# Attention with relative bias, then a snake MLP: the MLP lags one batch from the second batch on, and batch 1's attention output is transposed by DMA

## The chip, the cores and the metric

The kernel runs on one core of a Trainium2 chip. The metric is the device time of one execution in microseconds (us). The engines are TensorE (PE in the profile; PEld is its weight load), VectorE (DVE), ScalarE (ACT), GpSimd (POOL) and SyncE (SP), which here only issues DMAs. "Span" is the time from the first to the last instruction of the profiled execution.

## The reference

There are 8 batches of 8 heads, 576 positions and head size 64. All inputs are float32.

```python
scores = scale * np.matmul(q, k.transpose(0, 1, 3, 2))      # scale = 1/8
bias = bias_table[bucket]            # bucket depends on |i - j| alone, the last one from about 128 on
scores = scores + bias.transpose(2, 0, 1)[None, :, :, :]
scores = scores - np.max(scores, axis=-1, keepdims=True)
attn = np.exp(scores)
attn = attn / (np.sum(attn, axis=-1, keepdims=True) + 1e-09)
attn_out = np.matmul(attn, v)
...
x = np.ascontiguousarray(attn_out.transpose(0, 2, 1, 3)).reshape(B * S, H * D)   # 4608 x 512
h = x @ w_in                         # 512 -> 2048
s = np.sin(alpha * h)
g = h + s * s / (alpha + 1e-09)
return (g @ w_out).astype(np.float32)
```

## The kernel before

All matrix operands are float16. The attention works on one batch at a time and, within it, on four pairs of heads. The MLP works on nine blocks of 512 rows of x, which do not coincide with the 576 rows of a batch.

**Loads.** k and q of a batch from 2 on are first cast and rearranged from input to DRAM by GpSimd (`stage_kq`, two DMAs), and then loaded transposed into `kTs[t % 2]` and `qTs[t % 2]` by two DMA transposes on SyncE's queue, with two small copies of the last 64 keys into `kts` (`load_kqT`). v is loaded with a cast by six GpSimd DMAs (`load_v16`). For batch 2 the staging is issued in `first` of batch 0, and the loads in `first` of batch 1, which is executed where batch 1's first scores are emitted; there the staging of batch 3 follows on GpSimd's queue. For batches from 3 on, the function `ahead` (line 955) issues the loads, and the staging of the batch after, once the attention before last is finished. Batches 0 and 1 are loaded untransposed and transposed on TensorE (`plan_tr`).

**Attention.** `plan_qk` computes transposed scores: for a head pair p and a block i of 128 keys, two matmuls of 64 rows write one two-bank tile of PSUM; "t" is the last block of 64 keys of both heads together, and i = 4 the last 64 queries of four blocks. ScalarE takes the exponential into `u` (line 705), and VectorE multiplies it by the exponential of the bias near the diagonal (lines 713 and 730). `plan_av` multiplies `u` by v, to which a column of ones is attached, so that the sum of each row comes out too (24 exponentials, 36 product groups a batch). `norm` (lines 776 to 788) divides. The result must be transposed into `xT`, a ring of 1536 rows: for a batch that is not "far", TensorE transposes it (5 transposes for each head pair, line 822) and VectorE or ScalarE copies it (`put`, line 828); for a "far" batch `flip` (line 809) issues DMA transposes from `xp` on SyncE's queue. "Far" is `t >= LAG - 1`.

**PSUM.** Of eight banks, two are `am0` and `am1`, two each belong to regions R0 and R1 and two to region 2. Before batch LAG - 1 region 2 is two single banks, `ca` and `cb`, used by products, transposes and block 0's second matmul (tags "avE" and "moE"); scores then have two regions and are emitted tile by tile. From batch LAG - 1 on, region 2 is a third two-bank score tile (`c_mode` 2), and scores are emitted in the groups of lines 631 to 636, mostly two tiles at a time. The tile framework adds the waits where a region changes its form.

**MLP.** `plan_moe_in` computes h for a block in 16 tiles of four matmuls, in R0 and R1 with one bank each; ScalarE takes the sine, ScalarE or VectorE squares it, and VectorE makes g (line 879). `plan_mo` multiplies g by `w_out`: 4 x 16 matmuls for a block, called fills. Exponential and sine need different tables of ScalarE, so a switch costs an ACT_TABLE_LOAD, and the sines of a block wait for all exponentials ahead of them.

**Order.** `Plan.run` is a list scheduler that runs when the program is built. It takes the task that can start first by its own estimates of times; among those within 0.02 us it takes the one with the lowest priority number. The order in which it emits is the order of each engine's and each queue's program. Fills have the lowest urgency and fill gaps of TensorE; while scores of a batch are being emitted, `QUOTA` limits how many may go in: (a, b) allows a plus b times the share of the batch's score groups already emitted. Outside the scores they are not limited. The loop at line 945 plans, for each batch t, the attention, and then the MLP block `bs` of line 998; for t = LAG - 1 it plans no block, so that two attentions stand back to back. In the kernel before that is t = 2: the order is attention 0, block 0, attention 1, block 1, attentions 2 and 3, block 2, attention 4, block 3, and so on, and at the end blocks 6, 7 and 8. At t = LAG - 1 the tasks in `early` must also be done ahead of the first scores.

Of the kernel before, what the change touches and what calls it, by code (L numbers as in the profile page):

```python
# [20 lines left out]
def t_pe(n):  # L21
    return n / 2400.0 + 0.0025


def t_act(n):
    return n / 1200.0 + 0.052


def t_dve(n):
    return n / 960.0 + 0.07  # L30
# [141 lines left out]
WINDOW = 700  # L172
WARM_END = 30.0
FILL_GAP = 0.0
QUOTA = {2: (4, 26)}
QUOTA_ELSE = (8, 48)
LAG = 3
D_FLIP = 3.0
T_MODE = 0.11
T_START = 7.0  # L180
# [30 lines left out]
def kernel(  # L211
# [12 lines left out]
    T, H, S, D = q.shape  # L224
# [106 lines left out]
    def new_outs():  # L331
        return tp.tile([128, DM], F32, name="outs", tag="outs", bufs=NBUF["outs"])
# [29 lines left out]
    def bank(tag):  # L362
        if tag[:2] == "am":
            return new_ps(tag)
        n = its[tag]
        its[tag] += 1
        if tag == "avE":
            return new_c("ca") if n % 2 else new_ps("am0")
        if tag == "moE":
            return new_c("cb") if n % 2 else new_ps("am1")  # L370
        return new_c("ca" if n % 3 == 1 else "cb") if n % 3 else new_ps("am1")
# [3 lines left out]
    def stage_kq(t):  # L375
        for dst, src in ((staged_k, k), (staged_q, q)):
            nc.gpsimd.dma_start(  # L377
                out=dst.ap()[t].rearrange("s (h d) -> s h d", h=H),
                in_=src[t].rearrange("h s d -> s h d"),
            )  # L380
# [6 lines left out]
    def load_kqT(t):  # L387
        kT = kTs[t % 2]
        nc.sync.dma_start_transpose(out=kT[:, :, :], in_=staged_k.ap()[t])
        nc.sync.dma_start_transpose(out=qTs[t % 2][:, :, :], in_=staged_q.ap()[t])  # L390
        load_kt(t, 0, NP)

    def load_v16(t):
        vp = v[t].rearrange("h s d -> s h d")
        for c in range(4):
            nc.gpsimd.dma_start(  # L396
                out=vs[t % 2][:, c, :, 0:D], in_=vp[128 * c : 128 * c + 128],
            )
        vq = v[t].rearrange("(hp two) s d -> two s hp d", two=2)
        for z in range(2):  # L400
            nc.gpsimd.dma_start(
                out=vhs[t % 2][64 * z : 64 * z + 64, :, VC * z : VC * z + D], in_=vq[z, 512:S]
            )
# [45 lines left out]
    def full(out, lhsT, rhs, start, stop):  # L449
        nc.tensor.matmul(out=out, lhsT=lhsT, rhs=rhs, start=start, stop=stop)  # L450
# [83 lines left out]
    def copy_on(e, o, i):  # L534
        if e == "ACT":
            nc.scalar.activation(out=o, in_=i, func=AF.Copy)
        else:
            k_of(e).tensor_copy(out=o, in_=i)  # L538
# [84 lines left out]
    def plan_qk(t, deps, tails, first, gate, early):  # L623

        us, ubs = [Cell() for _ in range(NP)], [Buf("u") for _ in range(NP)]
        dones = [{} for _ in range(NP)]
        if t < LAG - 1:
            groups = [[(p, i)] for p in range(NP) for i in (0, 1, 2, 3, "t", 4)]
# [11 lines left out]
        for gi, g in enumerate(groups):  # L640
# [5 lines left out]
            def qk(e, gi=gi, g=g, scs=scs):  # L646
                if gi == 0:
                    first()
                    plan.in_qk, plan.used = True, 0
                    plan.quota = QUOTA.get(t, QUOTA_ELSE)  # L650
                plan.share = (gi + 1) / len(groups)
# [88 lines left out]
    avs, xps, xpn = {}, {}, {}  # L740

    def plan_av(t, p, w, u, ub, done):

        q0, n = WIN[w]
        nq = len(QC[w])
        at = "avE" if t < LAG - 1 else "am"
        ab, xb, tb = Buf(at), Buf("xn"), Buf(at)
        av, xn, tr = Cell(), Cell(), Cell()
        far = t >= LAG - 1
        if far:  # L750
# [86 lines left out]
    xdone = {}  # L837
# [65 lines left out]
    mo_last, cps = [], {}  # L903

    def plan_mo(b, a):

        mt = "moE" if b == 0 else "am" if b < T - 2 else "moL"
        mb, ob, m = Buf(mt), Buf("outs"), Cell()
        for f in range(NF):

            def mm(e, f=f):
                if f == 0:
                    m.v = bank(mb.tag)
                full(
                    m.v, gcell[b].v[:, f, 128 * a : 128 * a + 128], w_out16[:, f, :],
                    f == 0, f == NF - 1,
                )

            mo_last[:] = [plan.add({"PE": t_pe(512)}, mm, mo_last[:] + [gdone[(b, f)]],
                                   500000000 + 4 * b + a, nb=T_WO[f // 4] if b == 0 else 0.0,  # L920
                                   new=[mb] if f == 0 else [],
                                   use=[gbuf[b]] if f == 0 else [gbuf[b], mb])]
            mo_last[0].fill = True

        def cp(e):
            o = new_outs()
            copy_on(e, o, m.v)
            r0 = 512 * b + 128 * a
            nc.sync.dma_start(out=out[r0 : r0 + 128, :], in_=o)

        y = plan.add({"DVE": t_dve(512), "ACT": t_act(512)}, cp, mo_last[:], CP_PRI,
                     new=[ob], use=[mb])
        y.s_only = True
        cps.setdefault(b, []).append(y)

    def set_table(name):
        nc.scalar.preload_act_table_set(name)  # L937
        plan.sin = name == SIN_SET
# [6 lines left out]
    for t in range(T):  # L945
        PB = 1000000 * t

        def first(t=t):
            if t == 1:
                load_v16(t + 1)  # L950
                load_kqT(t + 1)
            if t < 2:
                stage_kq(t + 2)

        def ahead(e, t=t):
            load_kqT(t + 1)
            load_v16(t + 1)
            if t + 2 < T:
                stage_kq(t + 2)

        if 2 <= t < T - 1:
            aheads[t + 1] = plan.add({"SP": 0.1}, ahead, [], PB - 1000000,
                                     after=avs[t - 1] + xdone[(t - 1, 1)])
        if sins:
            gate = [plan.add({"ACT": D_TBL}, lambda e: set_table(EXP_SET), sins, PB)]
        sins = []
        deps, tails = [], []
        for p in range(NP):
            if t == 0 and p + 1 < NP:
                for kq in range(2):  # L970
                    tr[(0, p + 1, kq)] = plan_tr(0, p + 1, kq, 100 * (16 * p + 8), T_PAIR[p][kq])
            deps.append(pe_gate + (tr[(t, p, 0)][0] + tr[(t, p, 1)][0] if t < 2 else []))
            tails.append(tr[(t, p, 0)][1] if t < 2 else [])
            if (t, p) in split_of:
                tails[-1] = [split_of[(t, p)]]
        early = list(split_of.values()) if t == 1 else []
        if t in aheads:
            early = early + [aheads[t]]
        if t == LAG - 1:
            early = early + cps[0] + avs[1] + xdone[(1, 0)] + xdone[(1, 1)]  # L980

            def first(old=first):
                old()
                c_mode[0] = 2

        us, ubl, dones, exs = plan_qk(t, deps, tails, first, gate, early)
        exps = exps + exs
        for p in range(NP):
            for w in range(2):
                xdone.setdefault((t, w), []).extend(plan_av(t, p, w, us[p], ubl[p], dones[p]))  # L990
        if t == 0:
            for p in range(NP):
                for kq in range(2):
                    tr[(1, p, kq)] = plan_tr(1, p, kq, 20000 + 100 * kq + 10 * p, T_TR1[kq])
        if t == LAG - 1:
            continue
        tbl = [plan.add({"ACT": D_TBL}, lambda e: set_table(SIN_SET), exps, PB)]
        bs = [t] if t < LAG else [t - 1] if t < T - 1 else [t - 1, t, t + 1]
        for b in bs:
            m, s_ = plan_moe_in(b, tbl)  # L1000
            sins += s_
        exps = []
        pe_gate = [m]
        for b in bs:
            for a in range(4):
                plan_mo(b, a)
# [33 lines left out]
```

The softmax here doesn't subtract the row's maximum and nothing guards it: scores larger than these inputs give would overflow.

## Time and profile before

| what | us |
|---|---|
| median of 5 runs (range) | 392.82 (391.98 to 394.09) |
| the profiled execution, its own time | 392.62 |
| its span | 390.7 |
| PE busy | 377.3 (97%) |
| ACT busy | 323.6 (83%) |
| DVE busy | 262.2 (67%) |
| POOL busy | 81.8 (21%) |
| exponentials, line 705, 192 instructions | 157.4 |
| matmuls for h, 576 | 132.4 |
| products g, line 879, 144 instructions | 103.3 |
| sines, line 865, 144 instructions | 92.7 |
| transposes of x on TensorE, line 822, 40 | 5.0 |
| DMA transposes into xT, 64 | 2.9 each from issue to landing (median) |

A row of the page such as `PE 5989...` divides the span into 40 equal slices of 9.8 us; a digit is the busy share of a slice in tenths, 9 meaning 90% or more. In a timeline a row has start, duration, engine, line, operation, output<-input, shapes and a count; square brackets give the idle time before it and what ended it. Busy times of TensorE overlap at their ends, since a matmul of 512 columns starts every 0.216 us and is recorded with 0.38. Most matmuls carry line 450, that of a helper, so they are told apart by their tiles: `sc<-qT,kT` are scores, `am<-v,u` products with v, `sc<-xT,w_in` the h of the MLP, and `am<-w_out,g` (or `ca`, `cb`) fills.

### The profile page before, as it was taken

How to read it: one execution, taken by the hardware profiler on the slowest of the kernel's cores; microseconds unless marked ns; L12 is line 12 of the kernel's file. 1: busy time of each engine (PE TensorE's matmuls, PEld its weight loads, DVE VectorE, ACT ScalarE, POOL GpSimd, SP SyncE). 2: the span in 40 equal slices, each digit the busy share in tenths (PEclk: the TensorE clock that was granted, in tenths of full speed). 3: DMA queues.
4: the chain of work that ended last, by engine and by line, in shares of the span. 5: the costliest groups of instructions: out<-in, count | busy, mean ns of one | idle time of the engine just before them, and what ended most of it. 6: DMA issues, size and time to landing. Idle time of an engine off the chain costs nothing.

```text
span 390.7 us, 8566 instructions
## 1 busy us (share of the span) xinstructions
PE 377.3 (97%) x3401; PEld 189.4 (48%) x3401; DVE 262.2 (67%) x587; ACT 323.6 (83%) x458; POOL 81.8 (21%) x96
## 2 busy tenths in 40 slices
PE   5989999999999999999999999999999999999995
PEld 2466435644455554455445544564445444444442
DVE  3696977777676689667956895768676869429100
ACT  2886999988999999999989999999999969539211
POOL 5672863080005454002600400000000000000000
PEclk9999999999999999999999999999999999999999
DMA  9999999999928999992997498211014000020112
GB/s 169 210 208 219 207 172 144 167 152 132 147 67 90 155 153 161 158 155 54 141 167 107 60 67 187 59 21 42 29 42 60 17 28 29 27 81 2 61 73 81
DMA packets 148647, 41.99 MB, mean 107 GB/s; under 512 B 137784, under 2 KB 142992, under 8 KB 148608
## 3 DMA queue, kind: packets, MB, share of 16 engines
q0 software_dynamic: 89872, 19.04, 58.8%
q1 hardware_dynamic: 58512, 22.36, 31.4%
q8 instruction: 26, 0.43, 0.5%
q14 instruction: 13, 0.11, 0.1%
q10 hardware_dynamic: 224, 0.05, 0.1%
HBM read 37.76 MB, written 16.52 MB: 139 GB/s over the span
## 4 chain that ended last, share of the span: by engine, by line
PE 91%; ACT 4%; DVE 2%; DMA 1%; issue 1%; ACTq 0%; DVEq 0%
PE sc L450 44%; PE am L450 35%; PE cb L450 6%; PE ca L450 5%; ACT u L705 3%; DMA phi_sb<-phi_const 1%; PE cb L558 1%; DVE g L879 1%; PE am L558 1%; ACT s L865 1%; DVE kT L538 0%; DVE outs L538 0%; DVE xp L785 0%; PE ca L822 0%; ACT sq L872 0%
## 5 line engine op out<-in xcount | busy, mean ns | idle before, releaser
L705 ACT ACTIVATE u<-sc 128x1024 f16<-128x1024 f32 (+1 forms) x192 | 157.4, 898 | 12.8 <-PE sc L450 11.4
L450 PE MATMUL sc<-xT,w_in 128*128 128x512 f16 x576 | 132.4, 379 | 0.5 <-DVE g L879 0.5
L879 DVE SCALAR_TENSOR_TENSOR g<-sq,inv_a,sc 128x512 f16<-128x512 f16 x144 | 103.3, 746 | 22.0 <-PE am L450 14.7
L450 PE MATMUL am<-w_out,g 128*128 128x512 f16 x416 | 108.6, 380 | 0.3 <-DVE outs L538 0.2
L865 ACT ACTIVATE s<-sc,alphaT 128x512 f16<-128x512 f32 x144 | 92.7, 679 | 6.3 <-PE sc L450 4.8
L730 DVE TENSOR_TENSOR u<-u,m2r 128x512 f16<-128x512 f16 (+2 forms) x160 | 67.7, 438 | 30.9 <-ACT u L705 27.9
L450 PEld LDWEIGHTS <-w_in 128*128 128x128 f16 x576 | 55.2, 98 | 65.0 <-issue 1.6
L450 PEld LDWEIGHTS <-g 128*128 128x128 f16 x576 | 53.3, 98 | 64.1 <-issue 11.6
L450 PEld LDWEIGHTS <-u 128*128 128x128 f16 x1440 | 55.1, 97 | 18.7 <-issue 10.2
L450 PE MATMUL sc<-qT,kT 64*128 64x64 f16 (+1 forms) x512 | 50.3, 294 | 1.9 <-ACT u L705 0.9
L872 ACT ACTIVATE sq<-s 128x512 f16<-128x512 f16 x79 | 49.2, 628 | 2.3 <-DVE g L879 0.5
L450 PE MATMUL am<-v,u 128*128 128x65 f16 x1152 | 50.7, 193 | 0.0
L396 POOL DMA_DIRECT2D v<-in_v_dram x24 | 22.2, 1062 | 118.0 <-PE am L450 104.2
L874 DVE TENSOR_TENSOR sq<-s 128x512 f16<-128x512 f16 x65 | 27.4, 423 | 9.2 <-ACT s L865 8.8
L450 PE MATMUL am<-vh,u 128*128 128x130 f16 x144 | 32.1, 223 | 0.8 <-DVE xp L785 0.8
L450 PEld LDWEIGHTS <-kT 64*128 64x128 f16 x512 | 14.9, 95 | 28.6 <-issue 24.2
L785 DVE TENSOR_TENSOR xp<-am,rd 128x384 f16<-128x384 f32 (+1 forms) x48 | 23.6, 491 | 1.8
L784 DVE RECIPROCAL rd<-am 128x6 f32<-128x6 f32 (+1 forms) x56 | 10.5, 188 | 19.8 <-PE am L450 19.3
L450 PE MATMUL cb<-w_out,g 128*128 128x512 f16 x96 | 23.0, 379 | 0.0
L937 ACT ACT_TABLE_LOAD x13 | 16.7, 1283 | 0.2
L538 DVE COPY outs<-am 128x512 f32<-128x512 f32 x19 | 13.1, 688 | 4.3 <-PE am L450 4.1
L377 POOL DMA_DIRECT2D staged_q<-in_q_dram x6 | 15.1, 2515 | 3.7 <-DMA staged_q<-in_q_dram 3.7
(88 smaller groups left out, 175.2 us busy)
## 6 DMA issues: line engine op xcount, KB each, us to landing
out_dram<-outs SPq DMA_DIRECT2D x36, 256.0 KB, 2.2
staged_k<-in_k_dram POOLq DMA_DIRECT2D x6, 576.0 KB, 17.0
staged_q<-in_q_dram POOLq DMA_DIRECT2D x6, 576.0 KB, 21.8
v<-in_v_dram POOLq DMA_DIRECT2D x24, 128.0 KB, 8.3
w_in<-in_moe_w_in_dram POOLq DMA_DIRECT2D x4, 512.0 KB, 7.1
w_out<-in_moe_w_out_dram POOLq DMA_DIRECT2D x4, 512.0 KB, 10.9
w_out<-in_v_dram SPq DMA_DIRECT2D x4, 256.0 KB, 7.7
v1st<-in_v_dram POOLq DMA_DIRECT2D x4, 256.0 KB, 16.6
```

The costliest lines, as they stand in the source:

```text
L377: nc.gpsimd.dma_start(out=dst.ap()[t].rearrange("s (h d) -> s h d", h=H), in_=src[t].rearrange("h s d -> s h d"),)
L396: nc.gpsimd.dma_start(out=vs[t % 2][:, c, :, 0:D], in_=vp[128 * c : 128 * c + 128],)
L450: nc.tensor.matmul(out=out, lhsT=lhsT, rhs=rhs, start=start, stop=stop)
L538: k_of(e).tensor_copy(out=o, in_=i)
L705: nc.scalar.activation(out=o, in_=x, func=AF.Exp, scale=0.125)
L730: nc.vector.tensor_tensor(out=io, in0=io, in1=m2[:, 2 * p : 2 * p + 2, x0 : x0 + hi - lo], op=ALU.mult,)
L785: nc.vector.tensor_tensor(out=y.rearrange("p c (z d) -> p c z d", z=2), in0=a[:, :, :, 0:D], in1=r.unsqueeze(3).to_broadcast([128, nq, 2, ...
L865: nc.scalar.activation(out=s16.v, in_=h.v, func=AF.Sin, scale=alphaT[:, f : f + 1])
L872: nc.scalar.activation(out=sq.v, in_=s16.v, func=AF.Square)
L874: k_of(e).tensor_tensor(out=sq.v, in0=s16.v, in1=s16.v, op=ALU.mult)
L879: nc.vector.scalar_tensor_tensor(out=gcell[b].v[:, f, :], in0=sq.v, scalar=inv_a[:, f : f + 1], in1=h.v, op0=ALU.mult, op1=ALU.add,)
L937: nc.scalar.preload_act_table_set(name)
```

## The change

`LAG` becomes 2, and with it:

- The batch for which no block is planned is now t = 1. The order is attention 0, block 0, attentions 1 and 2, block 1, attention 3, block 2, and so on. From block 2 on it is that of before.
- Batch 1 becomes "far": its output is normalised into `xp` and transposed by DMA on SyncE's queue. Its scores are emitted in groups with three regions, and region 2 changes its form ahead of attention 1.
- The second matmul of block 0 uses `am0` and `am1` in place of `cb` and `am1`, since region 2 now belongs to scores.
- The first scores of batch 1, in place of those of batch 2, wait in the plan for the products and the transposed output of the batch ahead of them. They no longer wait for the output copies of block 0.
- The smaller quota (4, 26) for fills now holds for batch 1, and batch 2 has (8, 48).

```diff
@@ -172,9 +172,9 @@
-QUOTA = {2: (4, 26)}
+QUOTA = {1: (4, 26)}
 QUOTA_ELSE = (8, 48)
-LAG = 3
+LAG = 2
@@ -904,7 +904,7 @@
     def plan_mo(b, a):
 
-        mt = "moE" if b == 0 else "am" if b < T - 2 else "moL"
+        mt = "am" if b < T - 2 else "moL"
@@ -977,7 +977,7 @@
         if t == LAG - 1:
-            early = early + cps[0] + avs[1] + xdone[(1, 0)] + xdone[(1, 1)]
+            early = early + avs[t - 1] + xdone[(t - 1, 0)] + xdone[(t - 1, 1)]
```

## The prediction

> **What bounds the kernel now.** I read four views in this order: the page, the busy time of each engine by stage, the timelines of TensorE, ScalarE and the DMA queue of SyncE around the stages that move, and the landing times of the loads there. I write A0..A7 for the attention of a batch, M0..M8 for the first matmul of an MLP block with its sines, O0..O8 for its second matmul (64 fills each). From the page:
>
> ```profile
> PE   5989999999999999999999999999999999999995
> ACT  2886999988999999999989999999999969539211
> DMA  9999999999928999992997498211014000020112
> ```
>
> From slice 2 on TensorE is busy throughout, and in slices 0 to 10, up to 107 us, the 16 DMA engines are full. So time is won only by removing TensorE work or its hidden idling, and early on a load can be late. By stage, A1 | M1 | A2 | A3 | a later period (columns: stretch, its us, then PE, PEld, DVE, ACT, POOL busy with counts, clock, DMA):
>
> ```profile
> 53.45:78.73 25.28, 25.27 (x312) 14.19 (x312) 17.73 (x48) 24.33 (x33) 6.42 (x5) 1.00 2.08 157
> 78.73:98.04 19.31, 19.31 (x91) 8.61 (x90) 14.52 (x25) 16.28 (x26) 7.82 (x7) 1.00 1.96 140
> 98.04:117.97 19.93, 19.41 (x245) 10.17 (x244) 14.10 (x38) 19.14 (x24) 0.00 (x0) 1.00 0.87 103
> 117.97:137.66 19.69, 19.27 (x282) 10.76 (x281) 13.60 (x40) 18.34 (x24) 9.24 (x8) 1.00 1.42 126
> 257.33:297.83 40.50, 40.35 (x380) 20.02 (x378) 29.60 (x67) 38.74 (x55) 0.00 (x0) 1.00 0.20 42
> ```
>
> A1 and M1 are filled by TensorE. A2 and A3 look alike, but there ScalarE paces, as its timeline shows:
>
> ```profile
> 54.27 1.28 ACT L937 ACT_TABLE_LOAD   x1
> 55.57 14.05 ACT L705 ACTIVATE u<-sc 128x1024 f16<-128x1024 f32 x17
> ...
> 98.47 17.79 ACT L705 ACTIVATE u<-sc 128x1024 f16<-128x1024 f32 x22 [1.94 <-PE sc L450]
> ...
> 118.40 4.46 ACT L705 ACTIVATE u<-sc 128x1024 f16<-128x1024 f32 x5 [0.33 <-PE sc L450]
> ...
> 139.18 1.28 ACT L937 ACT_TABLE_LOAD   x1
> ```
>
> Exponentials run from 98.47 to 139.18 with only gaps of 0.2 to 0.33 us. TensorE's rows give the marks that I reuse:
>
> ```profile
> 94.27 3.62 PE L450 MATMUL cb<-w_out,g 128*128 128x512 f16 x16
> 97.73 0.38 PE L450 MATMUL am<-w_out,g 128*128 128x512 f16 x1
> 98.04 0.61 PE L450 MATMUL sc<-qT,kT 64*128 64x512 f16 x4
> ...
> 117.97 0.61 PE L450 MATMUL sc<-qT,kT 64*128 64x512 f16 x4
> ```
>
> First scores of A2 at 98.04, of A3 at 117.97 (19.93 later), M2's first matmul at 137.66 (19.69 later). The 16 fills in cb ahead of A2 finish O0, since A2 may not take the score region over before; ScalarE idles 1.94 us there. Last, the loads of batch 2 on SyncE's queue, and, from the answer on that one tile, the landing of q:
>
> ```profile
> 57.17 5.86 SPq L389 DMA_TRANSPOSE kT<-staged_k  x1
> 63.09 8.08 SPq L390 DMA_TRANSPOSE qT<-staged_q  x1
> 71.22 1.26 SPq L385 DMA_DIRECT2D kt<-kT  x2
> ```
>
> ```profile
> L390 SPq DMA_TRANSPOSE qT<-staged_q x1: 8082/8082/8082, 63.1 to 63.1; - x1
> DMA to landing us min/median/max: 14.8/14.8/14.8
> ```
>
> So q of batch 2 is in SBUF at 63.09 + 14.8 = 77.9. A2 asks for it at 98, 20 us later: today this costs nothing.
>
> **What the Trainium skill says.** "DMA: Bandwidth & Descriptors", section "Issuing engines are not separate DMA queues": transfers issued by different engines run on the same 16 DMA engines and interleave. The trace agrees: from 57 to 78 us the queues of POOL and SP together fill the engines, and the q transpose, which lands 4.9 us after issue in the emptiest part of the run, takes 14.8. "TensorE: Matmul & The Clock Gate", Part 1: a wholly idle window of about 3.4 us halves the clock. No stage after 53 us here shows this (clock 1.00); it matters for a rival. "ScalarE: Activation LUTs", "What ACT_TABLE_LOAD costs": 1283 ns a load; the page has 1283 for 13. Their number stays 13, as a pair of attentions without a switch between exists before and after.
>
> **The change, part by part.** Order before: A1, M1, A2, A3, M2, A4 ... After: A1, A2, M1, A3, M2, A4 ... Both contain one pair and the same stages from the pair on; the last batches are untouched.
>
> *Removed from A1.* 20 TensorE transposes (5 for each of 4 head pairs; by starts 0.22 + 0.21 us a pair, 1.7 us) and their copies: ScalarE 3 x 0.534 + 2 x 0.403 = 2.4 us, VectorE 0.351 + 2 x 0.258 = 0.9 us. The scores of A1 come in groups of two tiles: four matmuls in 0.54 us (98.04 to 98.58) where twice 0.33 (60.00 to 60.33) stood: 8 x 0.12 = 1.0 us less. All in A1, so 2.7 us of TensorE at most.
>
> *Moved out.* A2 no longer waits for O0's copies: the 1.94 us of idle ScalarE at 96.5 goes. A1 needs both of its first regions free, the second with the last product of M0, a VectorE row of 0.74 us from 54.64; so A1's first scores come at 55.4 instead of 53.45, with fills ahead of them. ScalarE's table is loaded until 55.55 anyway: free. Without that cover 2 us.
>
> *If no load were late:* A1 scores 55.4, A2 scores 55.4 + 19.93 = 75.3, M1 at 75.3 + 19.69 = 95.0.
>
> *The wait that appears.* A2's first scores read all of kT and qT of batch 2. SyncE issues those loads at the same place of its queue as before, at A1's first scores, and really starts when staged_k lands (issued at 44.85, 12.3 us). None of this is moved. So q is there at 77.9, and A2 starts at about 78.1, not 75.3: 2.8 us late. TensorE runs in order: behind these scores stand the last products of A1 with v, and behind them their normalisation and transposes; ScalarE has nothing else to do. Idle there is no longer made up, since both engines are about full after it. kts lands at 71.2 + 7.0 = 78.2, its second half about 0.6 later, and is read by A2's third group at about 80: not in the way. v of batch 2, issued from 48.3 to 50.9, lands by 69.3.
>
> *Added: flips.* 576 rows from row 576 don't cross row 1536 of xT, so a head pair takes 2 DMA transposes, 8 in all, about 1.3 us of SyncE each in busy stretches (138.11 to 149.22 for 8): 10.5 us. They queue behind the loads, from 72.5 on; the last pair's data exist at about 81, so its flips are issued by 84.5 and, at 8 us to land, are done at 93. M1 reads them at 97.8: hidden with 5 us to spare. The xp ring of 5 is reused by the second head pair of A2 at about 86, after the first flips land at about 83: free, by 3 us. The loads of batch 3, 76.97 before, come behind the flips at about 84.5; with the old delay of 20.7 us to q's landing they are in at 105 (kts 107), and A3 asks at 97.8 + 19.3 = 117. Free, by 10 us. v of batch 3 on POOL waits for A1's products, 77.1 before, 81 now, needed at 122. Output DMAs of O0 keep their size and number; each costs SP 0.35 to 0.56 us between flips. A missing cover would cost its lateness one for one.
>
> *Sum.* A2 at 78.1, M1 at 78.1 + 19.69 = 97.8, with O0 all done, as O1 is at M2 in the kernel before (137.66). From this point the kernel after runs what the other runs from M2, with one period more. The last such period takes 40.50 us and holds 62 fills of 64; two more at 0.216 us (17 fills, 94.27 to 97.94) make 40.9. Difference: 97.8 + 40.9 - 137.66 = +1.0 us. On the profiled execution's 392.62 this gives 393.6; the median of the runs shown is 0.2 higher, so 393.9 with a few tenths for the semaphore latencies left out.
>
> The removed TensorE work is not subtracted again: A1's length no longer counts, because the q load ends it. That is the choice on which this rests. Unknown sizes: the landing (77.2 to 79), A2's length after the start (18.9, were it ScalarE's 24 exponentials without the 0.2 to 0.33 us gaps, as fewer fills are left for A2; to 20.5), the extra period (40.5 to 41.3). Together -1.9 to +2.3 about the sum, if all fall one way.
>
> **The rivals.** *(A) Faster: the load is in time.* Place: first scores of A2. Without the wait the pair is paced by ScalarE alone: 95.0 + 40.9 - 137.66 = -1.8, so 391.1. Each us by which q lands earlier gives one us; break-even is a start of A2 at 77.1, so a landing of 76.9 instead of 77.9. For it: only 1 us of 14.8 decides, and A1's TensorE work is lighter. Against it: nothing ahead of this load in its queue is removed. *(B) Slower by more.* The wait of TensorE grows past its window and the clock halves: idle would be 2.8 us, near the 3.4 of the page named. Half a clock for 3.4 us loses 1.7 us of matmuls; with the flips holding up the batch-3 loads, or POOL, another 1 us: +2.5 to +3.7, 395.3 to 396.5. For it: full DMA engines until 107 us. Against: the margins above. *(C) Absorbed.* A2 catches up, since a part of the fills went into A1, and A3's 20.8 us of exponentials before included about 1 us of gaps: +0.0 to +0.3, 393.0. That the order is not as told, with A2's scores put later in TensorE's program by the planner, would look like (C) too.
>
> **How the numbers follow.** 0.3% is 1.2 us, about what a measurement of this kernel can tell from no change. Main case 0.56, with its own range from 393.0 to 395.2, a little over half of it above 394.0: 0.33 slower, 0.23 same. (A) 0.14 faster, (B) 0.19 slower, (C) 0.11 same. Slower 0.52, same 0.34, faster 0.14. The range 392.0 to 396.0 leaves out most of (A) and the upper part of (B).
>
> **What would show it.** Steps: A2's first scores preceded by idle TensorE and ScalarE of 2 to 3 us, the releaser the qT load landing near 78; exponentials of A1 over by 75.6; M1 from about 97.8 with no O0 left; xT copies gone from A1 and 8 flips between 72.5 and 85; M2 near 138. The prediction is wrong if A2's scores start before 77 (A), if A1 itself begins much after 56, if TensorE's matmuls after the wait take 0.43 us a start, or if A3's scores wait for their own load.

## The result, and the profile after

The changed kernel takes 395.59 us (median of 27 runs, 391.72 to 397.00) against 392.98 us (47 runs, 391.89 to 394.24) for the kernel before: a ratio of 1.0055, with a 95% interval from 1.0039 to 1.0071. It is slower, by more than the likeliest case had it (393.9), and its times are spread over 5.3 us where those of before lie within 2.4. They fall into two groups: six from 391.72 to 392.78, below the median of before, and 21 from 394.62 to 397.00. The profiled execution took 396.95 us, with a span of 395.2 against 390.7. One execution of the last variant below ran at a clock of 0.56 and took 628 us; it is left out of what is said there.

From the page of the kernel after, for comparison with the rows of before:

```profile
PE   5999999789999999999999999999999999999996
ACT  2876999769999999999999999999999958629211
PEclk9999999989999999999999999999999999999999
DMA  8999999999999949974996197120112000020122
```

There is a dip of TensorE and ScalarE in slice 7 (69 to 79 us), and in slice 8 the granted clock falls. By stage: A1 | the gap | A2 (columns as in the prediction):

```profile
56.58:75.95 19.37, 18.42 (x238) 9.86 (x238) 12.83 (x35) 18.89 (x24) 4.40 (x2) 1.00 1.98 144
75.95:80.47 4.52, 0.60 (x9) 0.13 (x5) 1.08 (x4) 0.69 (x2) 0.00 (x0) 1.00 1.94 175
80.47:101.05 20.58, 19.74 (x274) 11.61 (x274) 13.30 (x38) 17.97 (x23) 9.23 (x8) 0.92 1.68 153
```

In the second stretch both engines do 0.6 to 0.7 us of work in 4.5. The timeline of TensorE in the kernel after names what ended it:

```profile
75.95 0.59 PE L450 MATMUL am<-w_out,g 128*128 128x512 f16 x2
80.47 0.67 PE L450 MATMUL sc<-qT,kT 64*128 64x512 f16 x4 [3.92 <-DMA qT<-staged_q]
...
101.05 1.89 PE L450 MATMUL sc<-xT,w_in 128*128 128x512 f16 x8 [0.25 <-ACT u L705]
```

and that of ScalarE shows the same hole, with a second one behind it:

```profile
65.50 11.14 ACT L705 ACTIVATE u<-sc 128x1024 f16<-128x1024 f32 x14 [0.28 <-PE sc L450]
80.90 1.94 ACT L705 ACTIVATE u<-sc 128x1024 f16<-128x1024 f32 x2 [4.26 <-PE sc L450]
84.33 6.26 ACT L705 ACTIVATE u<-sc 128x1024 f16<-128x1024 f32 x8 [1.50 <-PE sc L450]
```

A1's exponentials are over at 76.6; A2's begin at 80.90. The second hole, of 1.50 us, was not forecast in the main case: for about 3.4 us after the wait, TensorE runs at half clock, so that eight of its products with v take 0.65 us where 0.41 stand before and after. On SyncE's queue:

```profile
59.00 6.01 SPq L389 DMA_TRANSPOSE kT<-staged_k  x1
65.07 8.61 SPq L390 DMA_TRANSPOSE qT<-staged_q  x1
73.73 1.25 SPq L385 DMA_DIRECT2D kt<-kT  x2
...
75.74 3.65 SPq L815 DMA_TRANSPOSE xT<-xp  x2
...
80.06 5.11 SPq L815 DMA_TRANSPOSE xT<-xp  x4
```

and of q alone:

```profile
DMA to landing us min/median/max: 15.3/15.3/15.3
```

The q load was issued at 65.07 and landed 15.3 us later, at 80.33; the first scores of A2 follow 0.14 us after it. The flips come where they were put, behind these loads.

### The profile page after: what moved, and what is told of

Same layout as the page of the kernel before. It is cut to its first block, busy times and chain, and to the rows that moved or that the text cites. A ratio compares the mean times of both kernels' runs of the same rounds, so it can differ in the third digit from the quotient of the medians.

```text
span 395.2 us, 8534 instructions
## 1 busy us (share of the span) xinstructions
PE 376.9 (95%) x3381; PEld 189.4 (48%) x3381; DVE 261.8 (66%) x584; ACT 322.4 (82%) x453; POOL 82.1 (21%) x96
## 4 chain that ended last, share of the span: by engine, by line
PE 83%; DMA 6%; ACT 4%; POOL 2%; DVE 2%; issue 1%; SPq 0%; ACTq 0%; DVEq 0%
PE sc L450 40%; PE am L450 34%; PE ca L450 4%; DMA qT<-staged_q 4%; ACT u L705 4%; PE cb L450 3%; DMA e_dram<-e_sb 1%; DMA phi_sb<-phi_const 1%; POOL v L416 1%; POOL m2r L464 0%; SPq L389 0%; DVE g L879 0%; DVE outs L538 0%; POOL vh L419 0%; POOL mhr L471 0%
## 5 line engine op out<-in xcount | busy, mean ns | idle before, releaser
L450 PE MATMUL am<-w_out,g 128*128 128x512 f16 x448 | 116.6, 381 | 0.3 <-DVE outs L538 0.2
L450 PEld LDWEIGHTS <-w_in 128*128 128x128 f16 x576 | 55.2, 98 | 64.6 <-issue 1.6
L450 PEld LDWEIGHTS <-u 128*128 128x128 f16 x1440 | 56.7, 99 | 17.8 <-issue 8.6
L450 PE MATMUL am<-v,u 128*128 128x65 f16 x1216 | 54.6, 195 | 0.0
L450 PE MATMUL am<-vh,u 128*128 128x130 f16 x152 | 34.2, 225 | 1.1 <-DVE xp L785 0.8
L785 DVE TENSOR_TENSOR xp<-am,rd 128x384 f16<-128x384 f32 (+1 forms) x56 | 27.5, 491 | 2.0
L538 DVE COPY outs<-am 128x512 f32<-128x512 f32 x21 | 14.4, 688 | 6.1 <-PE am L450 6.0
L536 ACT ACTIVATE outs<-am 128x512 f32<-128x512 f32 x7 | 4.2, 594 | 13.5 <-PE am L450 13.5
```

The costliest lines, as they stand in the source:

```text
L785: nc.vector.tensor_tensor(out=y.rearrange("p c (z d) -> p c z d", z=2), in0=a[:, :, :, 0:D], in1=r.unsqueeze(3).to_broadcast([128, nq, 2, ...
```

## The experiments

The theory: the start of A2 is the landing of batch 2's q; from there all runs as before, with one period more; and an idle TensorE may pay a stretch at half clock on top. The main rival: the other parts of the change, the flips, their DMA traffic and the three score regions, cost the time.

### The changed kernel again, three more profiles

No edit. The first comes with more executions, the other two are single profiled executions. The limit of 3.4 us in what was expected is the one that the prediction took from the page that it names.

> The changed kernel again, for more executions and a second trace beside its variants. Theory (the q load of batch 2 sets the start of attention 2): about +2 us against the kernel before; times fall into groups, and in the trace the first scores of attention 2 stand within 0.3 us of the landing of q of batch 2, wherever that is (77.5 to 81); the final time moves one for one with that landing, and where TensorE idled over 3.4 us a stretch at half clock follows. Rival (the DMA transposes of batch 1, or the shared score regions, cost the time): the time does not follow the landing.

> Another look at the changed kernel, for the relation of landing and time. Theory: span = (first scores of attention 2, within 0.3 us after the landing of q, not before 75.3) + 19.1 to attention 2's end where TensorE idled less than 3.4 us and the clock stayed whole, or + 20.6 to 21.0 where not, + 294.1. A landing of 77 so gives about 390.5, one of 79 with a whole clock 392.4, one of 80.3 with a stretch at half clock 395.2. Rival: the span does not come out of that sum within 0.6 us.

> The same once more, on the same terms: span = first scores of attention 2 + 19.1 (whole clock) or 20.6 to 21.0 (a stretch at half clock) + 294.1, within 0.6 us.

The first measured 396.03 us against 392.95, ratio 1.0073 (1.0049 to 1.0097). The first scores of A2, in the timelines of the three in turn:

```profile
80.03 1.04 PE L450 MATMUL sc<-qT,kT 64*128 64x512 f16 x4 [4.76 <-DMA qT<-staged_q]
```

```profile
78.78 1.03 PE L450 MATMUL sc<-qT,kT 64*128 64x512 f16 x4 [3.88 <-DMA qT<-staged_q]
```

```profile
77.96 0.61 PE L450 MATMUL sc<-qT,kT 64*128 64x512 f16 x4 [2.73 <-DMA qT<-staged_q]
```

Each stands 0.13 to 0.14 us after its landing (79.89, 78.65, 77.83). In the first two the four matmuls take 1.03 us, at half clock from the start; in the third they take 0.61, and the clock falls a little later. In the third, by stages of 2 to 3 us (the clock is the last column but two):

```profile
77.00:80.00 3.00, 2.04 (x26) 1.41 (x27) 0.42 (x1) 1.61 (x2) 0.00 (x0) 0.85 1.66 202
80.00:82.00 2.00, 2.00 (x17) 0.80 (x15) 1.22 (x3) 1.12 (x2) 0.00 (x0) 0.50 2.02 236
82.00:84.00 2.00, 2.00 (x33) 1.25 (x31) 1.02 (x3) 1.76 (x4) 0.32 (x1) 0.87 1.29 107
```

The clock is 1.00 on both sides of them, so half clock held for 2 x (3 x 0.15 + 2 x 0.50 + 2 x 0.13) = 3.4 us. The same working gives 6.8 us for the first two, of which some falls into the idle before the scores. All these profiles together, with those of the experiments below:

| run | q lands | first scores of A2 | half clock around it, about | A2 to M1 | M1 starts | span | span - M1 |
|---|---|---|---|---|---|---|---|
| kernel after, profiled | 80.33 | 80.47 | 3.4 | 20.58 | 101.05 | 395.2 | 294.1 |
| r1_after | 79.89 | 80.03 | 6.8 | 20.95 | 100.98 | 395.1 | 294.1 |
| r10_after_look | 78.65 | 78.78 | 6.8 | 21.70 | 100.48 | 394.6 | 294.1 |
| r11_after_look | 77.83 | 77.96 | 3.4 | 20.59 | 98.55 | 392.6 | 294.0 |
| r3_warm | 80.09 | 80.14 | none | 19.07 | 99.21 | 393.3 | 294.1 |
| r6_noflip | 76.99 | 77.12 | none | 19.24 | 96.36 | 391.3 | 294.9 |
| r2_scratch | not awaited | 75.25 | none | 19.07 | 94.32 | 388.6 | 294.3 |
| r5_gate | 71.50 | 75.32 | none | 19.07 | 94.39 | 388.5 | 294.1 |

The sum holds to 0.1 us for r11 (77.96 + 20.6 + 294.1 = 392.7). For r10 it fails by 0.7: the longer stretch at half clock lengthened A2 to 21.70, beyond the 21.0 that I had allowed. What follows M1 takes 294.0 to 294.3 us in all but one row; the 294.9 of r6_noflip comes up below.

No profile shows an execution of the faster group. By the sum, its fastest, with a span of 389.9, would have started A2 at 389.9 - 294.1 - 19.1 = 76.7, without a fall of the clock. This is an estimate; it fits the start of 77.12 in r6_noflip below.

### The wait taken away, its traffic kept

```diff
             if t == 1:
                 load_v16(t + 1)
-                load_kqT(t + 1)
+                for y, src in ((0, staged_k), (1, staged_q)):
+                    nc.sync.dma_start_transpose(
+                        out=v1st[:, NP * S * y : NP * S * (y + 1)].rearrange("p (h s) -> p h s", h=NP),
+                        in_=src.ap()[t + 1],
+                    )
```

> Batch 2's k and q are loaded by the same two DMA transposes at the same place, but into an unused tile, the two small copies of the last keys are left out, and attention 2 computes with batch 0's k and q, which are in their tiles already: all DMA traffic but 64 KB stays, the wait goes. Theory: no idle of TensorE over 1 us ahead of attention 2, its first scores at 75 to 77, and 391.2 us, that is -1.8 against before, with one group of times. Rival (flips, regions or DMA contention cost the time): still +1.5 or more against before.

390.94 us against 392.95, ratio 0.9944 (0.9929 to 0.9959). A2's scores start at 75.25, without a wait, in TensorE's timeline of this variant:

```profile
75.25 0.61 PE L450 MATMUL sc<-qT,kT 64*128 64x512 f16 x4
```

The same two transposes, the flips and the regions are all there, and the order is 2.0 us better than before: the rival falls. The prediction's 75.3 and -1.8 for a load in time are confirmed.

### The clock held, the wait kept

```diff
                     sc.v = new_sc(seq.index((p, i)) % nreg, 2)
+                    if t == 2 and gi == 0 and i == 0:
+                        for _ in range(14):
+                            full(sc.v[:, 0, :], zz[:, 0:128], zz, True, True)
```

> 14 matmuls on zeros (3.0 us) stand ahead of the first scores of attention 2, into the same bank, so that TensorE idles for less than 3.4 us at a stretch; the wait of the scores stays. Theory: the stretch at half clock after the wait goes, the wait itself stays; about 0.9 us less than the changed kernel in its slow group, median +1.0 to +1.6 against before. Rival (the half clock is the whole loss): 0 or less against before. Rival (the clock costs nothing, since ScalarE paces attention 2): no difference from the changed kernel.

394.39 us against 392.95, ratio 1.0035 (1.0025 to 1.0045): +1.4, and 1.6 less than the changed kernel on the same chip. TensorE's timeline of this variant:

```profile
75.86 3.19 PE L450 MATMUL sc<-zz 128*128 128x512 f16 x14
80.14 0.61 PE L450 MATMUL sc<-qT,kT 64*128 64x512 f16 x4 [1.09 <-DMA qT<-staged_q]
```

The load lands as late as in the changed kernel (80.09), but the clock stays at 1.00 and A2 lasts 19.07 in place of 20.6 to 21.7. So of the 5.1 us between the changed kernel and the variant without a wait (396.03 - 390.94), the clock is about 1.6 (396.03 - 394.39) and the wait itself about 3.5. With the 395.59 of the 27 executions, the clock's part is 1.2.

### Batch 2 staged earlier

```diff
-T_WO = (48.5, 50.5, 52.5, 54.0)
+T_WO = (48.5, 50.5, 58.5, 61.0)
...
-    load_w_out16()
+    load_w_out16((0, 1))
+    stage_kq(2)
+    load_w_out16((2, 3))
...
-            if t < 2:
+            if t == 1:
                 stage_kq(t + 2)
```

> The staging of batch 2 is put ahead of the second half of w_out in GpSimd's queue (w_out's later quarters are planned for 58.5 and 61.0), the rest is as in the changed kernel. Theory: k and q of batch 2 land about 5 us earlier, near 73 to 75, the wait in front of attention 2 vanishes, and the time is near that of the variant without the wait, -1 to -1.8 against before (391.2 to 392.0); fills come later, but a pair of attentions has room for them. Rival (the load is not the cause): +1.5 or more, plus what late fills cost.

395.26 us against 392.95, ratio 1.0054 (1.0034 to 1.0075): a miss. The number is that of the rival, but q lands at 75.73 and nothing waits for it any more; TensorE's timeline of this variant has the wait elsewhere:

```profile
60.64 1.03 PE L450 MATMUL am<-w_out,g 128*128 128x512 f16 x4 [1.21 <-DMA w_out<-in_moe_w_out_dram]
...
64.12 0.99 PE L450 MATMUL sc<-qT,kT 64*128 64x512 f16 x4
```

The last quarters of w_out land at 60.60 and 64.01, later than the plan was told, and fills put ahead of their weights hold TensorE, with a stretch at half clock after it. A second version tells the plan the measured times (61.5 and 65.0):

> As the variant with the staging of batch 2 ahead of the second half of w_out, but the plan now expects w_out's last two quarters at 61.5 and 65.0, where they landed, so that no fill is put ahead of its weights. Theory: no wait for q at 79, none for w_out at 60 to 64; 391.5 to 392.5 against before's 393. Rival (there is too little other work for TensorE from 55 to 65): it stays near 394 to 395, with ScalarE idle there.

393.69 us against 393.07, ratio 1.0012 (0.9998 to 1.0027): no difference from before, so a miss too. No instruction waits for w_out now, but from 56 to 63 there are no fills to put in, TensorE idles between ScalarE's exponentials, and its clock falls again (four scores take 1.03 us at 62.67). This fall follows no long idle. The longest ahead of it is 0.60 us, and in the 3.41 us before it TensorE is busy for 1.41, as the timeline and the sums of this variant show:

```profile
57.62 0.39 PE L450 MATMUL sc<-qT,kT 64*128 64x512 f16 x2 [0.60 <-ACT u L707]
```

```profile
55.95:59.36 3.41, 1.41 (x8) 0.58 (x8) 1.39 (x3) 3.40 (x5) 0.62 (x1) 1.00 1.28 200
```

The DMA engines are full in this stretch, and the transfer that was put ahead made another late: w_out's last quarter lands at 63.6 here and at 55.2 in the changed kernel.

### The traffic put off

The staging of batch 3 shares the DMA engines with the loads of batch 2 and isn't needed for a long time.

```diff
+    gsc = sgl.tile([128, 1], F16, name="gsc")
...
-            if t < 2:
+            if t == 0:
                 stage_kq(t + 2)
...
+        if t == 1:
+
+            def staged(e, u=us[3]):
+                nc.gpsimd.tensor_copy(out=gsc, in_=u.v[:, 0, 0:1])
+                stage_kq(3)
+
+            plan.add({"POOL": 0.2}, staged, [exs[18]], PB, use=[ubl[3]])
```

> The staging of batch 3 is held back on GpSimd until the fourth head pair of attention 1 has its first exponential (about 72 us), by a copy of one element that reads it; the rest is the changed kernel. Theory: what makes q of batch 2 late is the traffic that it shares the DMA engines with; with the staging of batch 3 out of the way from 70 on, q lands near 76 to 77 instead of 80, and each us earlier is a us less: 391.5 to 393 against before's 393 (-1.5 to 0), no stretch at half clock. v of batch 3 and its k and q come no later than needed (attention 3 at 115). Rival (the chain of issues on SyncE's queue sets the landing, not shared traffic): q still lands near 80, +2 to +3.

391.04 us against 393.07, ratio 0.9947 (0.9929 to 0.9966): faster than both kernels, and it leaves no work out. SyncE's queue in this variant, and the landing of q there:

```profile
57.53 5.91 SPq L390 DMA_TRANSPOSE kT<-staged_k  x1
63.49 6.07 SPq L391 DMA_TRANSPOSE qT<-staged_q  x1
```

```profile
DMA to landing us min/median/max: 8.0/8.0/8.0
```

With the issue at 63.49, like before's 63.09, q is there in 8.0 us in place of the 14.5 to 15.3 of the kernels before and after, earlier than I had expected of it (71.5, not 76). The two other variants with this edit, below, have 7.9 and 7.8. So the time from issue to landing was set by the traffic beside it, the staging of batch 3. A2 starts at 75.32, as in the variant that doesn't wait.

Does the later staging gain by itself? The same edit in the kernel before:

> The kernel before with the staging of batch 3 held back as in the variant of the changed kernel that was the fastest. Theory: the later staging gains only by the earlier landing of q of batch 2, for which this order does not wait: 393 within 0.8 us. Rival (less traffic in attention 1 speeds up other work too): 1 us or more faster than before.

393.17 us against 392.60, ratio 1.0004 (0.9992 to 1.0016). It brings nothing where nobody waits for q.

### The flips undone

```diff
-        far = t >= LAG - 1
+        far = t >= LAG
...
-            tr.v = bank(at).bitcast(F16)
+            tr.v = bank(tb.tag).bitcast(F16)
```

> The order of the changed kernel, but batch 1's output is transposed on TensorE and copied by VectorE and ScalarE, as before (with the two am banks); 8 DMA transposes fewer, 20 TensorE transposes more. Theory: in attention 1 this work is covered by the wait for q of batch 2, so the time is that of the changed kernel within 0.8 us, +2 to +3.5 against before; a part that falls after the wait (the last head pair) may cost up to 0.5. Rival (the DMA transposes lengthen the wait or hold up later loads): 1.5 us or more faster than the changed kernel.

396.77 us against 393.07, ratio 1.0069 (1.0044 to 1.0093), where the changed kernel has 1.0055 and 1.0073: no difference that these intervals show. Its times lie in two groups, 392.7 to 394.0 and 396.4 to 398.4. Group against group they are 1.0 to 1.1 us above those of the changed kernel (medians 393.1 against 392.0, and 397.5 against 396.5), which the overall medians do not show. The profiled execution is one of the first, with q at 76.99 and a wait of only 1.30 us, after which the clock stays whole:

```profile
77.12 0.61 PE L450 MATMUL sc<-qT,kT 64*128 64x512 f16 x4 [1.30 <-DMA qT<-staged_q]
```

With the wait gone:

> The fastest variant (staging of batch 3 held back), with batch 1's output transposed on TensorE and copied by VectorE and ScalarE. Without a wait for q nothing covers this work, and ScalarE paces the pair: theory +1.0 to +2.4 us against that variant (2.4 us of copies on ScalarE in attention 1 before, some of which VectorE takes), so 392 to 393.4, near the kernel before. Rival (the DMA transposes gain nothing, or cost as much as they save): 391 within 0.6.

391.76 us (21 executions) against 393.26, ratio 0.9968 (0.9955 to 0.9980), which is 0.8 us more than the same variant with flips (0.9947). The two intervals overlap a little, so this alone is a tendency; it has the size of the difference between the groups above. It is less than the 1.0 to 2.4 that I had worked out, and most of it is not the work of the transposes. In the traces M1 starts at 94.63 in place of 94.39, so within the pair the work is nearly absorbed, and at the last table load of ScalarE the two runs still differ by only 0.27 us (294.88 and 294.61). The span is 1.1 us longer all the same. TensorE's timelines show where the rest arises, without the flips and with them:

```profile
319.89 1.24 PE L451 MATMUL am<-w_out,g 128*128 128x512 f16 x5 [0.69 <-ACT outs L537]
```

```profile
313.59 6.42 PE L451 MATMUL am<-w_out,g 128*128 128x512 f16 x29
```

Without the flips 24 fills stand there, then 0.69 us of idle until ScalarE has copied an output away; with them 29 fills run through. r6_noflip has the same idle of 0.69 us at the same place, which accounts for most of its 294.9. So it belongs to another order of the matmuls late in these two programs; why the planner orders them so was not tested.

### The kernel before, profiled again

> A second look at the kernel before. Theory: q of batch 2 lands anywhere from 77.5 to 81 in it as well, since nothing ahead of that load differs, and it makes no difference there, as attention 2 asks at 98: 392 to 394. Rival (the change itself puts the load off): it lands at 78 again.

392.51 us; q lands at 79.00, and A2 asks for it at 98 again. So the 77.9 of the first profile is not a fixed time. In the profiles of the kernels before and after it is 77.8 to 80.3, and 77.0 without the flips. Most of this spread is older than the q load: in the four profiles of the changed kernel, SyncE's k transpose, which stands ahead of it, goes out between 57.00 and 59.00, as GpSimd issued the staging of batch 2 between 44.38 and 46.77. Whether the changed program as such shifts the landing by part of a microsecond, these few profiles don't say.

## Why the prediction was right or wrong

**The bound, and the new wait.** Right. A2's first scores wait for q of batch 2, whose place in SyncE's queue is the old one, and both engines are idle until it lands. A1 began at 56.58 in the first profile and at 54.94 to 55.30 in the other three, where the prediction had 55.4. Without the wait, the pair starts A2 at 75.25 to 75.32 (75.3 predicted) and the order gains 2.0 us (1.8 predicted).

**The sum.** In the profiled execution it came to +4.5 us of span, not +1.0. The terms: the landing, 80.3 where I took 77.9, +2.4; the length of A2, 20.58 where I took 19.69, +0.9; the extra period, 294.1 - (390.7 - 137.66) = 41.1 where I took 40.9, +0.2. In the medians it is +2.6.

*The landing* is the first term that was mis-sized. I read one time from one execution, of an interval in which the DMA engines are full, and allowed for 77.2 to 79. In four profiles of the changed kernel it was 77.8 to 80.3. Of the 2.4 us in the first of them, 2.0 were there when the q load was issued (65.07 against 63.09), and only the rest came from a longer way from issue to landing (15.3 against 14.8). Before the change this spread can't be seen in the time, since nobody waits for it; after it, the spread is handed on to the end, one us for one.

*The length of A2* hides two errors that partly cancel. Without a fall of the clock it is 19.07, not 19.69: nearer to the bound of 18.9 that I had kept for fewer fills. This fits the counts, 22 fills in that A2 of the variant without a wait against 29 in the A3 whose length I took; it was not tested apart. And with the fall it is 20.6 to 21.7.

**Rivals.** The clock was the mechanism of (B), at 1.7 us, and I left it out of the likeliest case because an idle of 2.8 us seemed too short. "TensorE: Matmul & The Clock Gate" speaks of one idle window of about 3.4 us. The runs show falls with 3.88 to 4.76 us of idle, but also with 2.73, with 1.21 as the longest (r4_early) and with 0.60 (r8_early2), and none with a single idle of 1.30 or 1.09. The measurement decides: the length of one idle is not what to go by, and the last section has what the runs show in its place. So leaving the clock out was the second misjudgement; the sign that the prediction had named for it, 0.43 us from one matmul to the next, came. The clock's price was about right: 1.2 to 1.6 us between the variants with and without. The other part of (B), held-up loads of batch 3, did not come: A3's first scores are at 120.27, and their q has landed at 109.2. (A) was right in its price and in its point, a start of A2 near 77 (r6, at 77.12, has a span 0.6 over before's, with the idle of 0.69 us near its end in it). It seems to have come in the six executions of the faster group, by the estimate above; reliably it comes only with the traffic moved. (C) did not happen.

**Flips.** Right that they are hidden. The 8 flips were issued between 75.7 and 91.4 and not between 72.5 and 84.5; they started 3 us later than told, as the queue ahead of them was 2 to 3 us later.

**Chances.** The direction, slower, was the likeliest of the three, and the range to 396.0 held the median, but the range of the main case alone, to 395.2, did not: the median belongs to a mixture of the main case and the clock of (B). That it stayed inside the range was in part luck: it moves with the share of executions whose load is in time, and the six executions of r1_after have a median of 396.03.

## What to carry to other kernels

When stages are put in another order, ask of every load what it was hidden under, and take its landing time as a range: where the DMA engines are full, the landing depends on what else is in flight, and on when the transfers ahead of it went out. Look next for traffic that isn't needed yet and hold it back; putting the late load ahead of other needed traffic only moved the wait. A short wait of an otherwise full TensorE can cost more than its length, as the clock may be halved for some us behind it, and so can a row of shorter ones.

## What the runs showed of the hardware

- The fall of TensorE's clock followed how busy TensorE had been over some us, and not the length of one idle. The granted clock, read in stretches of 0.5 us, gives the six falls between 50 us and the last matmuls in these traces. An edge inside a stretch is worked out from the mean clock there, as above; all times are in us.

| run | half clock | longest idle of TensorE ahead of the fall | busy in the 3.41 before the fall | busy in the first 3.41 after it |
|---|---|---|---|---|
| kernel after | 80.89 to 84.30 | 3.92 | 0.42 | 3.41 |
| r11_after_look | 79.12 to 82.53 | 2.73 | 1.16 | 3.41 |
| r4_early | 61.53 to 64.94 | 1.21 | 1.67 | 3.41 |
| r1_after | 77.40 to 84.23 | 2.1, going on | 1.27 | 0.79 |
| r10_after_look | 77.77 to 84.60 | 2.9, going on | 0.54 | 2.40 |
| r8_early2 | 59.36 to 66.19 | 0.60 | 1.41 | 2.80 |

- In all six TensorE was busy for less than half of the 3.41 us before the fall. In the 3.41 us ahead of those it was busy for 2.35 or more (r4_early has the least), and the clock did not fall. Where between the two the limit lies, these runs don't show.
- The clock came back after 3.41 us where TensorE was busy for the whole of them, and after 6.83 us where it was not. This is a pattern of six falls, which no run set out to test.
- A DMA transpose of 576 rows by 512 in float16 took 15.3 us to land, and held SyncE's queue for 8.6, next to the staging of batch 3 (kernel after); with that staging held back 8.0 and 6.1 (r5_gate). In the emptiest part of the run it had been 4.9 and 2.3 (the last such load of the kernel before, at 238 us).
